# A sparse attention and ELU block on one core: the second batch's attention pieces placed by a written list, and the opening and the load queue reordered

## The chip, the cores and the metric

The kernel runs on one core of a Trainium2 chip. The metric is the device time of the program in microseconds (us). Three runs of the kernel before took 324.32, 326.67 and 323.88 us; their median is 324.32 us.

## What is computed

Two stages follow each other. First attention over 8 batches, 8 heads, 576 positions and 64 values a head: the first four heads see the last 32 positions ("local"), the other four see earlier positions that are equal modulo 32 ("strided"). Then the 4608 rows of 512 values go through two matrix products with an ELU between them.

```python
def _attn_ref(q, k, v):
    B, H, S, D = q.shape            # 8, 8, 576, 64
    stride = 32
    scores = 1.0 / np.sqrt(D) * np.matmul(q, k.transpose(0, 1, 3, 2))
    pos = np.arange(S)
    rel = pos[:, None] - pos[None, :]
    mask_local = (rel >= 0) & (rel < stride)
    mask_strided = (rel >= 0) & (pos[None, :] % stride == pos[:, None] % stride)
...
    attn = np.exp(scores)           # of the masked scores, less their maximum
    attn = attn / (np.sum(attn, axis=-1, keepdims=True) + 1e-09)
    return np.matmul(attn, v)

def _moe_ref(x, w_in, w_out):       # w_in 512 x 2048, w_out 2048 x 512
    h = x @ w_in
    g = np.where(h > 0.0, h, np.exp(np.minimum(h, 0.0)) - 1.0)
    return g @ w_out
```

## The kernel before

Everything is issued in an order written out by the program; the engines' queues run in that order, and each instruction waits only for what it needs. So a piece that waits holds up all that is queued behind it on its engine.

**Pairs and pieces.** A batch's attention is four pairs of heads: strided s0 and s1, local l0 and l1 (capital S0 and S1 are the strided pairs of batch 1). A pair is a chain of pieces: `t_q` and `t_k` transpose queries and keys on TensorE into a PSUM bank, from which ScalarE or VectorE copies them to SBUF (L360 to L387); `s0` and `s1` are the scores' matmuls with the exponential on ScalarE and the mask on VectorE (L488 to L525); `a0` and `a1` multiply with the values, and VectorE takes a reciprocal and a product (L527 to L555); `x` transposes the result back and copies it into `xT`, the ELU part's input (L566 to L595). `v_in` copies strided values from `v_raw` to `v_str` (L416), and `halo` copies the overlapping rows of local values within `v_loc` (L423); the local `a` pieces need it. In `xT` the four blocks of 128 rows are c = 0 (l0), 1 (l1), 2 (s0) and 3 (s1).

**PSUM.** `pair_a` holds scores, three single banks rotate through transposes, products and x ("the ring"), and three banks (two halves and the fourth single) rotate through the ELU's input products; late in a chunk the fourth single goes to the output products (`share`, L115).

**The opening** is batch 0's attention, written as the list `OPENING`. `fill.n` are n matmuls whose result nobody uses (L724); `moe.c` are the first three output blocks' matmuls for one block c of `xT` (L633). Pieces named in `ON_VECTOR` are copied by VectorE, all others of batch 0 by ScalarE.

**The chunks.** Then nine chunks of 512 rows follow. Chunk nb has 16 steps m: four matmuls with `w_in` (L629), the exponential on ScalarE (L655), and on VectorE a step with the exponential (L662) and a maximum with the product (L664); in chunk 0, m = 4, 7, 10, 13 and 15 have a ReLU on ScalarE instead (L658) and one VectorE step (L659). The output products (L678, `outs`) of a chunk run mostly during the next. Between these stand the attention pieces of batch nb + 1, at gaps: gap 2m is ahead of step m, gap 2m + 1 behind it. `attention` (L597) puts them there from a row of `TIMES`: a start, a pitch between pairs, and eight offsets. For batch 1 this was start 3, pitch 6: S0.t_k at gap 1, S0.s0 at 3, S0.a0 at 7, S1.halo at 13, l0.a0 at 19, l1.x at 30.

**Loads.** All loads but the first are issued by GpSimd in program order (L309 to L346, L738 to L746): among them quarter i of `w_in` (512 columns, steps 4i to 4i + 3), batch 1's strided q, k and v, its local q, k and v, then the third and fourth quarter of `w_in`, four pieces of `w_out`, some clears, and batch 2's loads.

Of the kernel before, what the change touches and what calls it, by code (L numbers as in the profile page):

```python
# [32 lines left out]
PIECES = (-2, -1, 0, 2, 3, 5, 7, 0)  # L33
TIMES = (
    None,
    (3, 6, (-3, -2, 0, 2, 4, 6, 9, 3)),
    (4, 6, (-3, -2, 0, 2, 4, 6, 8, 0)),
    (2, 7, PIECES),
    ((2, 8, 15, 22), 0, PIECES),
)  # L40

OPENING = """
s0.cast_q s0.t_q s0.t_k s1.cast_q s1.t_k s0.s0 s0.m0 s1.t_q s0.s1 s0.m1 fill.2 l0.t_q s1.s1
s1.m1 s1.s0 s1.m0 l0.t_k l1.t_q fill.1 s0.v l0.s0 l0.m0 l1.t_k l0.s1 s1.a0 s0.a0 l0.m1 l1.s0
s1.a1 s0.a1 fill.1 l1.s1 l1.m0 fill.1 s1.halo s1.x fill.1 s0.x l1.m1 fill.1 l0.a0 fill.1 l0.a1
l1.a0 moe.2 l1.a1 S0.t_q l0.x S1.t_q moe.3 l1.x moe.0 moe.1
""".split()  # L50
ON_VECTOR = "s0.t_q s1.cast_q s1.t_k l0.t_q s0.v l1.x".split()


ON_SCALAR = (4, 7, 10, 13, 15)
# [4 lines left out]
def kernel(  # L59
# [9 lines left out]
    nc = tc.nc  # L69
    B, H, S, D = q.shape  # L70
# [44 lines left out]
    def share(sc, hps, ops, ring):  # L115
        rings.update(sc=Ring(*sc), hps=Ring(*hps), ops=Ring(*ops), ring=Ring(*ring))
# [9 lines left out]
    def bf16_bank():  # L126
# [14 lines left out]
    v_str = [consts.tile([128, 4, 5, D + 1], BF16, tag=f"v_str{i}", name=f"v_str{i}")  # L141
             for i in range(3)]
# [23 lines left out]
    raw = {}  # L166
# [21 lines left out]
    def load_local(b, name):  # L188
        if name == "v":

            nc.gpsimd.dma_start(
                out=v_loc[b % 3][32:128, :, :, :D].rearrange("p h i d -> p (h i) d"),
                in_=v[b, 0:4].rearrange("h (i p) d -> p (h i) d", p=LB))
            return
        flat = nat[name, "loc"][b % 3]
        if b < EARLY:
            nc.gpsimd.dma_start(
                out=flat[0:LB].rearrange("p (h x) -> p h x", h=4),
                in_=src[name][b, 0:4].rearrange("h (p j) d -> p h (j d)", j=L_RUN))
            return  # L200
        t = flat[:, 0:20 * D].rearrange("p (a i e d) -> p a i e d", a=2, i=5, d=D)
        for h in range(4):
            nc.gpsimd.dma_start(  # L203
                out=t[:, h // 2, 0:4, h % 2],
                in_=src[name][b, h, 0:512].rearrange("(i p) d -> p i d", p=128))
        for a in range(2):
            nc.gpsimd.dma_start(
                out=t[0:64, a, 4],
                in_=src[name][b, 2 * a:2 * a + 2, 512:576].rearrange("h p d -> p h d"))

    def transpose_batch(b, local):

        def strided():
            for name, to in (("q", qT), ("k", kT)):
                nc.sync.dma_start_transpose(out=to["str"][b % 2],
                                            in_=nat[name, "str"][b % 3])

        if BY_DMA <= b <= LATE and local < 2:
            strided()
        if b >= EARLY and local:  # L220
            for name, to, o in (("q", qT, 0), ("k", kT, 32)):
                for a in range(2):
                    nc.sync.dma_start_transpose(
                        out=to["loc"][b % 2][:, a, o:o + 640].rearrange(
                            "p (i r) -> p i r", r=128),
                        in_=nat[name, "loc"][b % 3][:, 640 * a:640 * a + 640])
        if b > LATE:
            strided()

    def load_batch(b):  # L230
        for name in "qkv":
            load_strided(b, name)
        for name in "qkv":
            load_local(b, name)

    def rows_of(t, h):

        return t[0:126, h, 0:2, :], t[0:108, h, 2:5, :]
# [83 lines left out]
    def load_w_in(i):  # L322
        nc.gpsimd.dma_start(out=w_in_sb[:, :, 512 * i:512 * (i + 1)],
                            in_=wi[:, :, 512 * i:512 * (i + 1)])
# [5 lines left out]
    load_strided(1, "v")  # L330
    load_local(1, "q")
    load_local(1, "k")
    load_local(1, "v")
    load_w_in(2)


    class Pair:
# [6 lines left out]

        def copy(self, step, late):

            if self.b == 0:
                late = f"{self.name}.{step}" in ON_VECTOR
            return nc.vector.tensor_copy if late else nc.scalar.copy

        def cast(self, name):
# [214 lines left out]
        def x_out(self):  # L566
# [22 lines left out]
            else:  # L589
# [4 lines left out]
                        identity[0:LB, 0:LB])  # L594
                self.copy("x", self.b > 1)(dst, xt[:, 0:S])  # L595

    def attention(b, start, pitch, at):  # L597


        gaps = {}  # L600
        pairs = [Pair(b, s, hp) for s in (b < LATE, b >= LATE) for hp in range(2)]
        begin = start if b >= LATE else [start + pitch * i for i in range(4)]
        if b >= LATE:
            gaps[begin[0]] = [pairs[3].halo]
        for i, pr in enumerate(pairs):
            if b == 1 and pr.strided:
                pr.t_q = lambda: None
            for off, piece in ((at[0], pr.t_q), (at[1], pr.t_k),
                               (at[7], lambda pr=pr: pr.v_in(0)),
                               (at[7] + (b > 1), lambda pr=pr: pr.v_in(1)),  # L610
                               (at[2], lambda pr=pr: pr.scores(0)),
                               (at[3] if b < WHOLE else at[2] + (b < LATE),
                                lambda pr=pr: pr.scores(1)),
                               (at[4], lambda pr=pr: pr.av(0)),
                               (at[5] - (b >= LATE and i == 0),
                                lambda pr=pr: pr.av(1)),
                               (at[6] + (b > 1 and pr.strided) + (b >= LATE), pr.x_out), (at[5] - 2, pr.halo if b < LATE else lambda: None)):
                gaps.setdefault(begin[i] + off, []).append(piece)
        return gaps
# [91 lines left out]
    def run(gaps, keys):  # L711
        for gap in sorted(g for g in gaps if g in keys):
            for piece in gaps[gap]:
                piece()

    every = range(-10, 1000)
    pairs = {p.name: p for p in (Pair(0, s, hp) for s in (True, False) for hp in range(2))}
    pairs.update((f"S{hp}", Pair(1, True, hp)) for hp in range(2))
    parts = [s for s in OPENING if s.startswith("moe")]
    for step in OPENING:  # L720
        pair, what = step.split(".")
# [29 lines left out]
    def outs(nb, s):  # L751

        if nb == 0:
            return [(0, i) for i in range(3) if s == 11 + 2 * i]
        step = [(nb - 1, i) for i in range(3, MC)]
        if nb < n_chunks:
            step += [(nb, i) for i in range(3)]
        else:
            step[0:2] = step[1::-1]
        return step[s:s + 1]  # L760

    for nb in range(n_chunks + 1):

        if nb + 1 < B:
            gaps = attention(nb + 1, *TIMES[min(nb + 1, 4)])
            if nb == 0:
                share([pair_a], b_halves + singles[3:], [], singles[:3])
            elif nb + 1 < LATE:
                share([pair_a], b_halves, singles[3:], singles[:3])
            else:  # L770
                share([pair_a], b_halves + singles[:1], singles[3:], singles[1:3])
        else:
            gaps = {}
            share([], b_halves + singles[:1], singles[2:], singles[1:2])
        if nb + 3 < B:
            load_batch(nb + 3)
        for s in range(MC):
            if nb == 0 and s == 10:
                share([pair_a], b_halves, singles[3:], singles[:3])
            if s == (9 if nb + 2 > LATE else 6) and nb > 0 and nb + 2 < B:  # L780
                transpose_batch(nb + 2, int(nb + 2 >= LATE))
            if s == 13 and nb + 2 == EARLY:
                transpose_batch(nb + 2, 2)
            run(gaps, (2 * s,) if s else range(-10, 1))
            late = LATE <= nb + 1 and s + 1 < MC
            if nb < n_chunks:
                moe_in(nb, s)
            if nb < n_chunks and not late:
                moe_act(nb, s)
            run(gaps, (2 * s + 1,) if s + 1 < MC else range(2 * s + 1, 1000))  # L790
            if nb < n_chunks and late:
                moe_act(nb, s)
            if nb == B and s == 4:
                range_flag(row_ok16)
            for chunk, i in outs(nb, s):
                moe_out(chunk, i)
        if nb + 1 == B:
            row_ok16 = range_check()
# [163 lines left out]
```

## Time and profile before

| what | us |
|---|---|
| median of three runs | 324.32 |
| the profiled execution | 324.63 |
| its span, first to last instruction | 322.7 |
| TensorE matmuls busy | 304.5 |
| VectorE busy | 244.9 |
| ScalarE busy | 175.9 |
| GpSimd busy | 140.1 |

Times are from the start of the span. The profile's names: PE is TensorE's matmuls, PEld its weight loads, DVE is VectorE, ACT is ScalarE, POOL is GpSimd, SP is the queue that issues the output's transfers. `L629` is line 629 of the kernel before. In the timeline a line gives the start, the duration, the engine, the line, the operation with output and input, and in brackets how long the engine stood idle before and who ended that. A block of matmuls is shown with the last one's way through the array, so the next block may start before it ends. "Granted clock" is the share of full speed that TensorE was given.

Where the stages lie in the profiled execution: the opening to 27.3, chunk 0 from there to 55.8 (its first matmuls, the last `moe` of the opening, at 26.66), chunk 1 from 55.76 to 91.69.

### The profile page before, as it was taken

The numbers are of one execution on the slowest core, as the hardware profiler recorded it, in microseconds if no ns is written. First come the engines' busy times: TensorE is split into PE (matmuls) and PEld (weight loads), VectorE is DVE, ScalarE is ACT, GpSimd is POOL, SyncE is SP. The second block draws the span as 40 slices with busy tenths as digits, with TensorE's granted clock in tenths as the row PEclk, the third lists the DMA queues.
The fourth block names the chain that finished last, engine by engine and source line by source line (L and its number), as shares of the span: only waits on it lengthen the run. The fifth ranks groups of instructions, "written<-read, shape, count | busy, mean of one in ns | idle before, by whom it ended". The sixth has DMA issues, their size and how long they took to land.

```text
span 322.7 us, 6076 instructions
## 1 busy us (share of the span) xinstructions
PE 304.5 (94%) x2214; PEld 151.6 (47%) x2214; DVE 244.9 (76%) x539; ACT 175.9 (55%) x334; POOL 140.1 (43%) x218
## 2 busy tenths in 40 slices
PE   1997988999999999999999999999999999999994
PEld 0564444555544544444444444444444444444443
DVE  6576887787888988989798879887988566776610
ACT  3668885776555554555555565565555534434411
POOL 9859725958957839978942840000000000000000
PEclk9999899999999999999999999999999999999999
DMA  6999999999999999999994994291110000010012
GB/s 108 159 174 121 168 207 138 145 134 174 90 149 176 141 141 186 77 159 168 196 134 102 125 208 95 71 152 58 54 51 34 35 32 35 37 62 34 35 67 72
DMA packets 108970, 36.33 MB, mean 113 GB/s; under 512 B 87357, under 2 KB 104453, under 8 KB 108933
## 3 DMA queue, kind: packets, MB, share of 16 engines
q0 software_dynamic: 71632, 18.10, 62.4%
q1 hardware_dynamic: 37301, 17.77, 26.9%
q8 instruction: 19, 0.31, 0.4%
q14 instruction: 18, 0.15, 0.1%
HBM read 36.70 MB, written 9.44 MB: 143 GB/s over the span
## 4 chain that ended last, share of the span: by engine, by line
PE 85%; DVE 6%; ACT 3%; DMA 2%; issue 1%; POOL 1%; ACTq 0%; POOLq 0%
PE single L678 37%; PE half L629 27%; PE single L629 9%; PE single L542 3%; PE pair_a L463 2%; ACT e_sb L655 2%; PE single L382 2%; DMA k_str<-in_k_dram 2%; DVE g_sb L664 1%; DVE x_l L551 1%; PE single L578 1%; DVE e_sb L662 1%; PE single L368 1%; PE pair_a L500 1%; PE single L724 1%
## 5 line engine op out<-in xcount | busy, mean ns | idle before, releaser
L678 PE MATMUL single<-w_out_sb,g_sb 128*128 128x512 bf16 (+1 forms) x592 | 145.9, 373 | 0.0
L629 PE MATMUL half<-xT,w_in_sb 128*128 128x512 bf16 x436 | 113.4, 382 | 0.0
L655 ACT ACTIVATE e_sb<-half 128x512 f32<-128x512 f32 x109 | 65.3, 599 | 69.7 <-PE half L629 67.4
L662 DVE TENSOR_SCALAR e_sb<-e_sb 128x512 bf16<-128x512 f32 x139 | 64.0, 460 | 36.0 <-ACT e_sb L655 34.9
L678 PEld LDWEIGHTS <-g_sb 128*128 128x128 bf16 x592 | 55.2, 98 | 57.6 <-DVE g_sb L664 0.2
L629 PEld LDWEIGHTS <-w_in_sb 128*128 128x128 bf16 x576 | 52.0, 98 | 56.7 <-issue 2.2
L664 DVE TENSOR_TENSOR g_sb<-e_sb,half 128x512 bf16<-128x512 bf16 x104 | 71.5, 688 | 3.7
L629 PE MATMUL single<-xT,w_in_sb 128*128 128x512 bf16 x140 | 36.5, 379 | 0.0
L655 ACT ACTIVATE e_sb<-single 128x512 f32<-128x512 f32 x35 | 21.0, 600 | 24.2 <-PE single L629 22.0
L683 ACT COPY o_sb<-single 128x512 f32<-128x512 f32 (+1 forms) x37 | 21.3, 576 | 17.0 <-PE single L678 16.7
L542 PEld LDWEIGHTS <-pr 128*128 128x128 bf16 (+3 forms) x352 | 21.0, 106 | 15.6 <-issue 0.9
L469 ACT ACTIVATE pr<-pair_a 126x936 bf16<-126x936 f32 (+1 forms) x20 | 19.2, 962 | 12.5 <-PE single L463 12.5
L180 POOL DMA_DIRECT2D k_str<-in_k_dram x32 | 20.7, 662 | 10.7 <-DMA w_in_sb<-in_moe_w_in_dram 3.0
L664 DVE TENSOR_TENSOR g_sb<-e_sb,single 128x512 bf16<-128x512 bf16 x35 | 24.1, 688 | 1.2
L180 POOL DMA_DIRECT2D v_raw<-in_v_dram x32 | 19.9, 648 | 9.4 <-DVE v_str L421 7.5
L180 POOL DMA_DIRECT2D q_str<-in_q_dram x28 | 17.6, 650 | 6.4 <-DMA w_in_sb<-in_moe_w_in_dram 1.9
L551 DVE TENSOR_TENSOR x_l<-single,rden 96x384 bf16<-96x384 f32 x32 | 17.7, 553 | 1.1
L551 DVE TENSOR_TENSOR x_s<-single,rden 126x256 bf16<-126x256 f32 (+1 forms) x32 | 15.7, 491 | 1.1
L203 POOL DMA_DIRECT2D q_loc<-in_q_dram x20 | 15.5, 817 | 2.3 <-PE single L382 0.8
L203 POOL DMA_DIRECT2D k_loc<-in_k_dram x20 | 15.8, 820 | 0.7 <-DMA q_loc<-in_q_dram 0.5
L508 ACT ACTIVATE pr<-pair_a 128x576 bf16<-128x576 f32 (+2 forms) x20 | 13.0, 652 | 5.6 <-PE pair_a L500 5.5
L550 DVE RECIPROCAL rden<-single 96x6 f32<-96x6 f32 (+2 forms) x64 | 11.9, 185 | 3.3 <-PE single L542 2.7
(114 smaller groups left out, 261.6 us busy)
## 6 DMA issues: line engine op xcount, KB each, us to landing
out_dram<-o_sb SPq DMA_DIRECT2D x35, 256.0 KB, 3.1
v_loc<-in_v_dram POOLq DMA_DIRECT2D x8, 288.0 KB, 7.9
k_str<-in_k_dram POOLq DMA_DIRECT2D x32, 67.5 KB, 5.0
v_raw<-in_v_dram POOLq DMA_DIRECT2D x32, 67.5 KB, 4.7
w_in_sb<-in_moe_w_in_dram POOLq DMA_DIRECT2D x4, 512.0 KB, 10.0
w_out_sb<-in_moe_w_out_dram POOLq DMA_DIRECT2D x4, 512.0 KB, 16.5
q_str<-in_q_dram POOLq DMA_DIRECT2D x28, 67.5 KB, 7.2
q_loc<-in_q_dram POOLq DMA_DIRECT2D x20, 64.0 KB, 4.4
```

The lines of the kernel that those rows point to most:

```text
L180: engine.dma_start(out=t[0:108, h].rearrange("p g d -> p (g d)"), in_=rows[h, :, 0:30, :].rearrange("t (r g) d -> t r (g d)", g=5))
L203: nc.gpsimd.dma_start(out=t[:, h // 2, 0:4, h % 2], in_=src[name][b, h, 0:512].rearrange("(i p) d -> p i d", p=128))
L469: nc.scalar.activation(both, sc[0:nk, :, 0:w], ACT.Exp, scale=scale)
L508: nc.scalar.activation(halves, sc[0:nk, :, 0:w], ACT.Exp, scale=scale)
L542: nc.tensor.matmul(av[0:m, p, blk - b0, :], lhsT=pr[0:nk, o:o + m], rhs=vt[0:nk, 2 * self.hp + p, blk, :], start=True, stop=True)
L551: nc.vector.tensor_tensor(self.x[0:nq, b0:b0 + n].rearrange("q g p d -> q p g d"), av[0:nq, :, 0:n, 0:D], r.unsqueeze(3).to_broadcast([nq, ...
L629: nc.tensor.matmul(hps, lhsT=w_in_sb[:, c, m * 128:(m + 1) * 128], rhs=xT[:, c, nb * N_TILE:(nb + 1) * N_TILE], start=start, stop=stop)
L655: nc.scalar.activation(e_sb, hps, ACT.Exp)
L662: nc.vector.tensor_scalar(e1_sb, e_sb, scalar1=1.0, scalar2=1.0, op0=ALU.min, op1=ALU.subtract)
L664: nc.vector.tensor_tensor(g_of[nb][:, m, :], e1_sb, hps, op=ALU.max)
L678: nc.tensor.matmul(ops, lhsT=g_of[nb][:, m, kk * 128:(kk + 1) * 128], rhs=w_out_sb[:, m, cols], start=(m == 0), stop=(m == MC - 1))
L683: nc.scalar.copy(o_sb, ops)
```

## The change

`OPENING`: `s1.halo` stands ahead of l1.s1, `l0.a0` ahead of s0.x, `S0.t_q` behind `moe.3`, and two of eight fills are gone. S1.t_q's copy goes from ScalarE to VectorE. Batch 1's pieces in chunk 0 stand in a list, `SECOND`, with a gap for each, and no longer come from `TIMES`; its local pairs have their transposes there too. The copies of batch 1's strided values go from ScalarE, at gap 6, to GpSimd, in its queue behind the load of the local values. The third quarter of `w_in` is loaded ahead of the local values. Batch 2 starts at gap 5, not 4. The first three output pieces of chunk 0 follow steps 12, 14 and 15, not 11, 13 and 15, and the fourth single bank changes hands at step 11, not 10.

```diff
 TIMES = (
     None,
-    (3, 6, (-3, -2, 0, 2, 4, 6, 9, 3)),
-    (4, 6, (-3, -2, 0, 2, 4, 6, 8, 0)),
+    None,
+    (5, 6, (-3, -2, 0, 2, 4, 6, 8, 0)),
...
+SECOND = """
+3 S0.t_k 5 S0.s0 7 S0.s1 8 S1.t_k 9 S1.s0 11 S0.a0 11 S1.s1 12 S0.a1 13 S1.a0 14 l0.t_q
+15 S1.a1 15 S0.x 16 l0.t_k 17 l1.t_q 18 S1.x 18 l0.s0 19 l1.t_k 20 l0.s1 21 S1.halo 21 l1.s0
+22 l0.a0 24 l0.a1 24 l1.s1 26 l1.a0 26 l0.x 27 l1.a1 30 l1.x
+""".split()
...
-s1.a1 s0.a1 fill.1 l1.s1 l1.m0 fill.1 s1.halo s1.x fill.1 s0.x l1.m1 fill.1 l0.a0 fill.1 l0.a1
-l1.a0 moe.2 l1.a1 S0.t_q l0.x S1.t_q moe.3 l1.x moe.0 moe.1
+s1.a1 s0.a1 s1.halo fill.1 l1.s1 l1.m0 fill.1 s1.x l0.a0 l1.m1 fill.1 s0.x l0.a1 l1.a0 moe.2
+l1.a1 l0.x moe.3 S0.t_q l1.x S1.t_q moe.0 moe.1
 """.split()
-ON_VECTOR = "s0.t_q s1.cast_q s1.t_k l0.t_q s0.v l1.x".split()
+ON_VECTOR = "s0.t_q s1.cast_q s1.t_k l0.t_q s0.v l1.x S1.t_q".split()
...
     load_local(1, "k")
+    load_w_in(2)
     load_local(1, "v")
-    load_w_in(2)
+    for o, i in zip(rows_of(v_str[1][:, :, :, 0:D], slice(0, 4)),
+                    rows_of(raw[1], slice(0, 4))):
+        nc.gpsimd.tensor_copy(o, i)
...
-            if self.b == 0:
-                late = f"{self.name}.{step}" in ON_VECTOR
+            if self.b < 2:
+                name = self.name.upper() if self.b else self.name
+                late = f"{name}.{step}" in ON_VECTOR
             return nc.vector.tensor_copy if late else nc.scalar.copy
...
+    def second():
+        pairs.update((f"l{hp}", Pair(1, False, hp)) for hp in range(2))
+        gaps = {}
+        for gap, step in zip(SECOND[::2], SECOND[1::2]):
+            pair, what = step.split(".")
+            gaps.setdefault(int(gap), []).append(
+                lambda p=pairs[pair], what=what: p.step(what))
+        return gaps
...
-            return [(0, i) for i in range(3) if s == 11 + 2 * i]
+            return [(0, i) for i in range(3) if s == (12, 14, 15)[i]]
...
-            gaps = attention(nb + 1, *TIMES[min(nb + 1, 4)])
+            gaps = attention(nb + 1, *TIMES[min(nb + 1, 4)]) if nb else second()
...
-            if nb == 0 and s == 10:
+            if nb == 0 and s == 11:
                 share([pair_a], b_halves, singles[3:], singles[:3])
```

More of the change, by code (lines that the diff above doesn't have):

```diff
@@ L605, in attention @@
         for i, pr in enumerate(pairs):
-            if b == 1 and pr.strided:
-                pr.t_q = lambda: None
             for off, piece in ((at[0], pr.t_q), (at[1], pr.t_k),
```

## The prediction

> **What bounds the kernel now.** I began with the busy tenths over the span and the granted TensorE clock, from the profile's page.
>
> ```profile
> PE   1997988999999999999999999999999999999994
> ...
> PEclk9999899999999999999999999999999999999999
> ```
>
> One slice is 8.07 us. From the eighth slice on TensorE is full; what an order can win lies before 56 us, where the change's edits lie too. Busy time by stretch sharpens that (columns: PE, PEld, DVE, ACT, POOL busy with counts, clock, DMA share, GB/s):
>
> ```profile
> 16.00:24.00 8.00, 7.54 (x89) 4.96 (x86) 6.40 (x21) 5.29 (x11) 4.04 (x7) 1.00 1.29 174
> 24.00:32.00 8.00, 5.76 (x54) 3.43 (x54) 5.12 (x10) 6.58 (x12) 7.92 (x13) 0.95 1.01 120
> 32.00:40.00 8.00, 7.59 (x80) 4.04 (x77) 6.68 (x16) 6.43 (x13) 6.33 (x10) 0.84 1.63 167
> 40.00:48.00 8.00, 6.69 (x82) 3.59 (x77) 6.94 (x18) 6.96 (x15) 1.90 (x3) 1.00 1.24 207
> 48.00:56.00 8.00, 7.16 (x54) 3.68 (x53) 6.21 (x14) 5.00 (x9) 4.22 (x8) 1.00 1.04 143
> ```
>
> TensorE idles 0.46 + 2.24 + 0.41 + 1.31 + 0.84 = 5.3 us between 16 and 56, and in windows of 1 us the clock is 0.61, 0.50, 0.50, 0.68 from 31 to 35, which is 1.7 us of full clock lost. No engine is full: VectorE and ScalarE reach 87% at the densest, from 40 to 48. So the stage is bound by in-order queues waiting for each other. The timeline shows with whom:
>
> ```profile
> 24.01 0.41 PE L591 MATMUL single<-identity,x_l 96*128 96x96 bf16 x6 [0.24 <-DVE x_l L551]
> ...
> 24.70 0.43 PE L368 MATMUL single<-identity,q_str 126*128 126x126 bf16 x5 [0.28 <-DVE x_l L551]
> ...
> 28.52 0.28 PE L500 MATMUL pair_a<-qT_str,kT_str 64*128 64x126 bf16 x4 [0.78 <-ACT kT_str L371]
> ...
> 31.27 0.43 PE L542 MATMUL single<-v_str,pr 126*128 126x65 bf16 x4 [0.48 <-ACT v_str L421]
> ...
> 36.05 1.16 POOL L245 MEMSET q_str<- 32x1280 bf16 x1
> ...
> 36.72 0.77 DVE L662 TENSOR_SCALAR e_sb<-e_sb 128x512 bf16<-128x512 f32 x1
> ...
> 42.62 0.32 PE L578 MATMUL single<-identity,x_s 108*128 108x108 bf16 x3 [0.69 <-DVE x_s L551]
> ```
>
> Last, the landings of the third and fourth quarters of w_in:
>
> ```profile
> L323 POOL DMA_DIRECT2D w_in_sb<-in_moe_w_in_dram x2: 790/796/803, 29.7 to 30.4; - x2
> ...
> DMA to landing us min/median/max: 10.2/11.1/11.9
> ```
>
> 29.7 + 10.2 = 39.9 for the third quarter, and m=8, its first user, starts at 40.06: no slack. By the same view k_loc lands at 35.0, v_loc at 37.8, the fourth quarter at 42.3, w_out's pieces at 45.0, 47.5, 50.1 and 52.7: one after the other, with 203 to 213 GB/s from 37 to 51 us.
>
> **The opening.** Two of eight fills go. In place one takes 0.39 (19.04 to 19.43; 21.32 to 21.71), 0.78 for both; waits in the stretch are 0.23 + 0.24 + 0.28 = 0.75; so at most 1.5. Against it: the halo copy (1.27 on ScalarE) now stands ahead of l1.s1's exponential and delays it by 0.2 (19.14 to 19.33; v_loc landed by 18.1). I walked the new order with the old durations, three banks in rotation: l0.a0 at 19.9 (was 21.12), l1.a0 21.4 (22.29), moe.2 21.85 (22.48; its quarter lands at 21.5), VectorE's last product ends 23.65 (24.65), moe.1 starts 25.55 (26.66). Gain **1.1**, bounds 0.6 and 1.5. S1.t_q's copy (0.68 on ScalarE, 25.18 to 25.86) goes to VectorE (0.47 by the row of s0.t_q), idle from 24.65 to 26.15: nothing on the path, since ScalarE's first exponential waits for moe.1.
>
> **The list, to m=8.** Start to start, from the timeline: exponential 0.49, ReLU 0.48, local copies and exponentials 0.53, strided x copies 0.59; on VectorE the ELU's two steps 0.46 + 0.60, its ReLU form 0.61, a mask 0.36 to 0.41, reciprocal and product 0.67 to 0.70; four 512-column matmuls 0.86; m's first matmul to its exponential 1.13, exponential to VectorE 0.63. With S0.t_k at gap 3, S0.s0 waits for its copy behind exp1 (start 27.75, was 28.52), then TensorE has m=3 and S0.s1 to run on. VectorE from 26.7 on: six ELUs 6.36, two ReLU forms 1.22, four masks 1.54, four products 2.75, in all 11.9 with almost no wait, so S1.a1 ends at 38.7 (was 42.5, the halo among it). S0.x waits for a bank that S1.a0's product frees, 37.5; m=8 starts at 38.07 (was 40.06). The third quarter, now ahead of v_loc, lands 2.1 to 2.5 behind k_loc, at 37.1 to 37.5: it fits by half a microsecond. In the old order it would hold m=8 to 39.9.
>
> **From m=8 on.** ScalarE starts S0.x's copy at 37.95 and then has l0.t_k, exp8, l1.t_q, S1.x, l0.s0, exp9, l1.t_k, l0.s1, exp10, ReLU10 without a gap: end 44.0. S1.halo, now at gap 21, is queued on VectorE behind m=10's last step (44.0 to 44.6) and takes 0.49; l0.a0 needs it: 45.1, was 44.12. TensorE has only l1.s0 in hand from 42.62 to 45.13, so the halo costs 1.8. m=11 then starts 45.45 (46.21), m=15 53.1 (54.03), the next chunk 54.83 (55.76): gain 0.9, opening included; without the halo's wait 2.7. v_loc lands at about 40.1, under both. Between these ends I take 1.9: that wait hangs on ten ScalarE pieces in a row, and some follow each other closer (43.48 to 43.56 for the second x copy); 0.1 each brings 1.0 back.
>
> **The v copies on GpSimd.** Rows near: a memset of 1280 elements 1.16; this copy on ScalarE 0.63 + 0.83. I take 1.3, bounds 0.9 and 2.5. They start at 30.4 (v_raw lands by 30.2), ready 31.7; S0.a0, now at gap 11, wants them at 32.0, so beyond 1.6 they cost one for one, to 0.9. Queued behind them are the fourth quarter, w_out, the clears and batch 2's loads: 1.3 later issue, hidden because the transfers ahead run to 40. Beside that q_str memset VectorE's L662 took 0.77, where its median in this stretch is 0.44: 0.34 lost. The walk leaves VectorE 0.25 idle near 31.7, waiting for ReLU4, so **0.1** is charged, bounds 0 and 0.7. The Trainium skill (SBUF — State Buffer, "Who interferes with whom") says that GpSimd and some VectorE forms take one port pair exclusively, the later one waiting the whole instruction; it adds reads of two SBUF inputs, as the masks have, once GpSimd itself reads. The 0.77 agrees with the first; no row shows the second.
>
> **Outs, share, start 5.** The outs move behind one more gap; each is 0.86 wherever it stands. Its pieces have landed by then. m=10 takes the same bank in either ring, as all are old. Start 5 puts the second chunk's pieces one gap later; TensorE is full there, so nothing, save at its end: l1.x falls on gap 31, behind m=15, and its VectorE copy behind m=15's ELU. From m=15's first matmul the copy ends at 1.13 + 0.63 + 1.06 + 0.45 = 3.25; TensorE has m=15, the transposes, an out and three of four matmuls of the next m=0, 0.86 + 0.27 + 0.86 + 0.65 = 2.64. It waits **0.6**, and nothing later makes that good (bounds 0 and 0.7).
>
> **Sum.** 1.9 − 0.1 − 0.6 = 1.2. The profiled execution took 324.63 (span 322.7 and 1.9 around it), so 323.4; the three runs' median is 0.31 lower: **323.1**.
>
> **Rivals.** (a) The halo's wait throws the clock, and it is slower. Before 31 us TensorE was busy 1.53 of 3 us (27 to 30), and 3.4 us at half clock followed. In my walk 42.6 to 45.1 is emptier. With the full wait (gain 0.9 − 0.1 − 0.6 = 0.2) and half clock over m=11, m=12 and the first out, 1.7 of work is lost: 324.3 − 0.2 + 1.7 = **325.8**. It decides where TensorE's busy share over some 3.4 us falls to about half; against it, such a stretch may straddle two windows. The Trainium skill (TensorE: Matmul & The Clock Gate, Part 1) has the gate look at free-running windows of about 3.4 us; the trace's 3.4 us at half agrees, and which stretch is hit would then differ from run to run. Chance 0.17. (b) Every cover holds: no halo wait, no stall at the second chunk's end, 2.7 − 0.1: **321.7**. Its floor is batch 2's loads, pinned behind w_out (the k_str row pieces issue at 52.9, then v_raw to 57.9, landing about 60.6; its copy on VectorE, was second at 63.43, can come at most 2.8 earlier without waiting), so 320.9. For it: TensorE's 5.3 idle. Against: VectorE's 11.9 us in a row. 0.22. (c) The opening's gain becomes waiting on VectorE: full halo wait, 0.7 beside GpSimd, 0.6 at the end, −0.4: **324.7**. 0.14. My forecast, 322.2 to 324.2, keeps 0.47.
>
> A measurement of this kernel tells about 1% (3.2 us) from no change. Faster than 321.1 needs (b) and its floor: 0.09. Slower than 327.6 needs (a) with a second half-clock spell: 0.05. Within: 0.86. The range runs from (b)'s floor, 320.9, to (a), 325.8, leaving out half of (a) and the tails.
>
> **What would show it.** moe.1 near 25.5; m=8 near 38.1 with no wait for w_in; l0.a0 waiting on the halo copy of VectorE at about 43 to 45; the first out's piece at 47 or later; a wait at the second chunk's end on x_l's copy; clock rows between 26 and 50. I am wrong if S0.a0 waits for GpSimd, if m=8 waits for its quarter, or if batch 2's k_str stops TensorE after 55.

## The result, and the profile after

The changed kernel takes 329.21 us in the median of six runs (325.89, 326.62, 329.15, 329.28, 329.46, 330.04), the kernel before 324.51 in six beside it. The ratio is 1.0143, 95% interval 1.011 to 1.0177: slower by 1.4%, where I had forecast a gain of 0.4%. The measured time lies above my range. Here and below a ratio leaves out the few runs that are over 1.5% above the fastest of the same kernel (one of e6, two of the kernel before beside e9 to e11).

The profiled execution of the changed kernel took 325.89, with a span of 323.8; it is the quickest of its six. Its page, the same two rows as before:

```profile
PE   1878678999999999999999999999999999999994
...
PEclk9999989999999999999999999999999999999999
```

The thin slices are now the third, fifth and sixth from the start, and the half clock has moved from the fifth slice (31 to 35 us) to the sixth. The same stretches as before, with the same columns:

```profile
16.00:24.00 8.00, 6.14 (x93) 4.29 (x96) 7.09 (x22) 5.57 (x11) 5.43 (x10) 1.00 1.34 182
24.00:32.00 8.00, 6.55 (x62) 3.30 (x61) 6.53 (x12) 6.77 (x13) 7.53 (x11) 1.00 1.04 124
32.00:40.00 8.00, 5.59 (x81) 3.39 (x78) 6.67 (x17) 5.07 (x11) 7.59 (x12) 1.00 1.71 169
40.00:48.00 8.00, 5.66 (x57) 2.96 (x58) 5.52 (x11) 5.10 (x12) 2.29 (x4) 0.84 1.24 207
48.00:56.00 8.00, 7.06 (x56) 3.81 (x58) 6.18 (x14) 4.78 (x9) 4.56 (x8) 0.95 1.04 140
```

From 32 to 48 TensorE is busy 11.3 of 16 us, where it was 14.3. The timeline names the waits (columns as before; L646 is now the first product, L553 the product with the values, L602 the local x):

```profile
20.11 0.30 PE L553 MATMUL single<-v_loc,pr 128*128 128x65 bf16 x4 [0.67 <-ACT v_loc L439]
...
25.07 0.59 PE L646 MATMUL half<-xT,w_in_sb 128*128 128x512 bf16 x2
...
34.86 0.45 PE L393 MATMUL single<-identity,q_loc 96*64 96x96 bf16 x12 [1.14 <-DVE x_s L562]
...
37.57 0.41 PE L589 MATMUL single<-identity,x_s 126*128 126x126 bf16 x5 [1.08 <-DVE x_s L562]
...
38.29 1.04 PE L646 MATMUL single<-xT,w_in_sb 128*128 128x512 bf16 x4
...
45.57 0.40 PE L553 MATMUL single<-v_loc,pr 128*128 128x65 bf16 x4 [1.75 <-DVE v_loc L439]
45.78 1.90 PE L646 MATMUL half<-xT,w_in_sb 128*128 128x512 bf16 x4
...
92.44 0.30 PE L602 MATMUL single<-identity,x_l 96*128 96x96 bf16 x3 [0.51 <-DVE x_l L562]
```

The opening's last matmuls start at 25.07 (26.66 before), m=8 starts at 38.29 with no wait for its quarter of w_in, l0.a0 waits 1.75 for the halo copy, and m=11 right behind it runs at half clock, 1.90 for four matmuls. In the last line, at the end of chunk 1, l1.x of batch 2 waits for a product, where before it went through at once (89.70, 0.42 for all six).

| point reached, us | before | changed | changed, once more (e1) |
|---|---|---|---|
| moe.1 starts | 26.66 | 25.07 | 25.00 |
| chunk 1 starts | 55.76 | 56.27 | 55.11 |
| chunk 2 starts | 91.69 | 93.44 | 92.17 |
| span | 322.7 | 323.8 | 322.4 |

So in the profiled execution the opening gives 1.6, chunk 0 takes 2.1, chunk 1 1.2, and 0.65 comes back later, most of it a wait of 0.60 at 133.35 that the changed kernel's profile does not have. That makes 1.1, and the other runs are up to 4 us longer.

The 1.6 is not all due to the new opening. In both profiles TensorE begins slowly and speeds up, at different times; this is a fill of 512 columns near 18 us, before and changed:

```profile
18.13 0.61 PE L724 MATMUL single<-mask_l,identity 128*128 128x512 bf16 x1
```

```profile
18.20 0.39 PE L741 MATMUL single<-mask_l,identity 128*128 128x512 bf16 x1
```

Before, matmuls take the long time until 20.8; in the changed kernel's profile only until about 15. The granted clock is 1.00 there in both, so it does not show this. The section on the prediction compares like with like.

Part of what the longer runs hold shows in their granted clocks: with each run's span and mean clock, the time at half clock is 2 x (1 − clock) x span. It is 5.2, 2.6, 9.2, 3.3, 12.4 and 8.5 us for the six in the order of their times, where runs of the kernel before have 2.8 in the mean (the 73 runs beside the experiments below). A spell, below, is a stretch at half clock.

### The profile page after: what moved, and what is told of

The parts are those of the page before. It is cut to its first block, busy times and chain, and to the rows that moved or that the text cites. A ratio compares the mean times of both kernels' runs of the same rounds, so it can differ in the third digit from the quotient of the medians.

```text
span 323.8 us, 6033 instructions
## 1 busy us (share of the span) xinstructions
PE 298.6 (92%) x2171; PEld 150.0 (46%) x2212; DVE 245.4 (76%) x540; ACT 172.7 (53%) x331; POOL 140.3 (43%) x220
## 4 chain that ended last, share of the span: by engine, by line
PE 78%; DVE 10%; ACT 4%; POOL 3%; issue 2%; DMA 2%; ACTq 0%; DVEq 0%; POOLq 0%
PE single L695 36%; PE half L646 25%; PE single L646 9%; DVE g_sb L681 3%; PE single L553 3%; DVE e_sb L679 2%; PE pair_a L474 2%; DMA v_raw<-in_v_dram 2%; ACT e_sb L672 2%; DVE x_l L562 1%; PE single L589 1%; DVE x_s L562 1%; DVE pr L534 1%; POOL k_str L187 1%; PE single L602 1%
## 5 line engine op out<-in xcount | busy, mean ns | idle before, releaser
L695 PE MATMUL single<-w_out_sb,g_sb 128*128 128x512 bf16 (+1 forms) x571 | 142.8, 373 | 1.6 <-issue 0.8
L646 PE MATMUL half<-xT,w_in_sb 128*128 128x512 bf16 x424 | 111.7, 382 | 1.0 <-issue 0.5
L679 DVE TENSOR_SCALAR e_sb<-e_sb 128x512 bf16<-128x512 f32 x139 | 64.0, 460 | 37.5 <-ACT e_sb L672 36.9
L695 PEld LDWEIGHTS <-g_sb 128*128 128x128 bf16 x592 | 54.5, 98 | 56.3 <-DVE g_sb L681 0.4
L646 PEld LDWEIGHTS <-w_in_sb 128*128 128x128 bf16 x576 | 53.0, 98 | 57.8 <-issue 1.5
L646 PE MATMUL single<-xT,w_in_sb 128*128 128x512 bf16 x134 | 35.7, 379 | 0.3
L553 PEld LDWEIGHTS <-pr 128*128 128x128 bf16 (+3 forms) x352 | 20.5, 103 | 16.9 <-issue 3.6
L187 POOL DMA_DIRECT2D q_str<-in_q_dram x28 | 18.3, 679 | 5.3 <-DMA w_out_sb<-in_moe_w_out_dram 1.9
L210 POOL DMA_DIRECT2D k_loc<-in_k_dram x20 | 15.1, 776 | 1.2 <-issue 0.7
L553 PE MATMUL single<-v_loc,pr 128*128 128x65 bf16 x192 | 11.9, 198 | 2.8 <-DVE v_loc L439 1.8
```

The source lines that it names most:

```text
L187: engine.dma_start(out=t[0:108, h].rearrange("p g d -> p (g d)"), in_=rows[h, :, 0:30, :].rearrange("t (r g) d -> t r (g d)", g=5))
L210: nc.gpsimd.dma_start(out=t[:, h // 2, 0:4, h % 2], in_=src[name][b, h, 0:512].rearrange("(i p) d -> p i d", p=128))
L553: nc.tensor.matmul(av[0:m, p, blk - b0, :], lhsT=pr[0:nk, o:o + m], rhs=vt[0:nk, 2 * self.hp + p, blk, :], start=True, stop=True)
L646: nc.tensor.matmul(hps, lhsT=w_in_sb[:, c, m * 128:(m + 1) * 128], rhs=xT[:, c, nb * N_TILE:(nb + 1) * N_TILE], start=start, stop=stop)
L679: nc.vector.tensor_scalar(e1_sb, e_sb, scalar1=1.0, scalar2=1.0, op0=ALU.min, op1=ALU.subtract)
L695: nc.tensor.matmul(ops, lhsT=g_of[nb][:, m, kk * 128:(kk + 1) * 128], rhs=w_out_sb[:, m, cols], start=(m == 0), stop=(m == MC - 1))
```

## The experiments

Each is timed beside runs of the kernel before; ratios are to those. The runs are 4 to 12 each; e1 to e4 share 15 runs of the kernel before, e5 to e8 another 29, e9 to e11 another 29.

| run | what | ratio | 95% interval | mean us at half clock |
|---|---|---|---|---|
| e1 | changed kernel again | 1.0128 | 1.0093 to 1.0164 | 7.2 |
| e2 | S1.halo at gap 19 | 1.0068 | 1.0039 to 1.0097 | 4.5 |
| e3 | batch 2 from gap 4 | 1.0095 | 1.0061 to 1.0129 | 7.0 |
| e4 | values on ScalarE | 1.0101 | 1.0042 to 1.0161 | 3.6 |
| e5 | before, new opening | 0.9995 | 0.9965 to 1.0025 | 4.5 |
| e6 | changed, waits filled | 1.0058 | 1.0027 to 1.0090 | 1.9 |
| e7 | before, list and outs | 1.0107 | 1.0065 to 1.0148 | 4.7 |
| e8 | e2 and e3 together | 1.0020 | 0.9990 to 1.0051 | 3.5 |
| e9 | before, opening and load order | 0.9975 | 0.9946 to 1.0004 | 3.8 |
| e10 | e9, a wait filled | 0.9958 | 0.9936 to 0.9981 | 1.9 |
| e11 | e8, a wait filled | 1.0007 | 0.9978 to 1.0037 | 2.2 |

**e1, the changed kernel once more.** No edit.

> The changed kernel once more, nothing edited. The runs already taken fall in two groups, 325.9 to 326.6 and 329.2 to 330.0, and the trace of the first group is known: l0.a0 waits 1.75 us for the halo copy, a spell at half clock follows from 45.8, the next chunk's last local transposes wait for a product. Theory A (the halo and the clock spell make the loss, and the second group has one more clock spell): a run near 329.5 shows the same waits and two stretches of half clock. Rival B (a lock or a late load after 55 us): a run near 329.5 shows the same first 56 us and loses its 3 us later, in a wait on VectorE, on GpSimd or on batch 2's loads.

Five runs from 324.52 to 328.47; the traced one is the shortest. Its clock row from the page, and its wait from the list of what TensorE waited for (total us, times, longest):

```profile
PEclk9999999999999999999999999999999999999999
```

```profile
PE single L553 <- DVE v_loc L439: 1.8, 1, 1.8
```

The same wait of 1.8, and no half clock up to the last slice. So the wait is there without the spell behind it, and the spell differs from run to run of one program. From the start of m=8 to that of chunk 1 this trace takes 16.74 us (38.37 to 55.11), the kernel before 15.70. Three traces with the wait and a spell of about 3.4 us, the changed kernel's, e4's and e7's, take 17.95 to 18.01; e3's, with the wait and a spell of 6.8, takes 19.43. So the new order with its wait costs 1.0 here, and each 3.4 us at half clock 1.2 to 1.4 more. The other four runs have 5.2 to 11.1 us at half clock and take 2.5 to 4.0 us longer. No run near 329.5 was traced, so what was asked of such a run stays unanswered; rival B finds nothing in this trace after 56 us but the end of chunk 1.

GpSimd's copies are slower in this trace than in the changed kernel's profile, and TensorE waits for them:

```profile
30.93 2.94 POOL L344 COPY v_str<-v_raw 126x512 bf16<-126x512 bf16 x2
```

```profile
33.92 0.36 PE L553 MATMUL single<-v_str,pr 108*128 108x65 bf16 x6 [1.38 <-DVE g_sb L681]
```

The list of waits names a VectorE step that ends at the same moment, but S0.a1 does not need that step: in the changed kernel's profile it runs at 32.32, ahead of it. It needs the second copy, which ends at 33.87. The wait is made good before m=8, which starts at 38.37, 0.08 later than in the other profile.

**e2, the halo earlier.**

```diff
-18 S1.x 18 l0.s0 19 l1.t_k 20 l0.s1 21 S1.halo 21 l1.s0
+18 S1.x 18 l0.s0 19 l1.t_k 19 S1.halo 20 l0.s1 21 l1.s0
```

> The changed kernel with S1.halo at gap 19 (behind m=9) in place of 21 (behind m=10). Theory A: the wait of 1.75 us at l0.a0 goes but for some 0.3, the half clock spell behind it goes too, and the kernel gains 2.5 to 3.5 us on the changed one: 323 to 326.5 by group. Rival B (the loss lies after 55 us): it gains under 1 us, as the later stretch waits for batch 2's loads whatever comes before. Rival C (v_loc lands too late at 40.1): VectorE waits for v_loc at gap 19 and nothing is gained.

Against e1, by the ratios, it gains 0.6%, 1.9 us, under what I asked of theory A and twice rival B. The wait is 0.2 in its trace, so v_loc is there in time and rival C is out. But that trace is at half clock for about 6.8 us, now earlier, as its busy times by stretch show (the same columns, the clock third from the end):

```profile
36.00:40.00 4.00, 2.92 (x23) 1.34 (x20) 2.40 (x6) 2.32 (x5) 3.54 (x4) 0.62 2.44 134
40.00:44.00 4.00, 4.00 (x40) 1.95 (x39) 1.57 (x3) 2.65 (x6) 1.17 (x2) 0.53 1.24 207
```

Ahead of it lie the waits at l0.t_q and S0.x (1.2 and 1.1 here). The list has two thin stretches, and either can be hit.

**e3, batch 2 from gap 4.**

```diff
-    (5, 6, (-3, -2, 0, 2, 4, 6, 8, 0)),
+    (4, 6, (-3, -2, 0, 2, 4, 6, 8, 0)),
```

> The changed kernel with batch 2's pieces from gap 4 again, as before the change. My theory of the second chunk's end: l1.x back at gap 30 takes back the 0.5 us wait of its transposes and the wait of the next chunk's first block, 1.0 to 1.3 us in all, unless batch 2's keys, landing near 57, stop TensorE at S0.t_k, which then costs up to 1 us. Expected 0.5 to 1.3 us faster than the changed kernel. Rival: start 5 is what keeps TensorE from waiting for batch 2, then 0 to 1 us slower.

1.1 us better than e1 by the ratios and 0.6 by the medians, with intervals that overlap; the trace decides. Chunk 1 runs there from 58.05 to 93.97, 35.92 us; before 35.93; the changed kernel 37.17 and, in e1, 37.06. So start 5 costs 1.15 to 1.25. The end of the chunk in e3's timeline, TensorE alone:

```profile
91.98 0.42 PE L602 MATMUL single<-identity,x_l 96*128 96x96 bf16 x6
92.24 1.03 PE L646 MATMUL half<-xT,w_in_sb 128*128 128x512 bf16 x4
93.97 1.03 PE L646 MATMUL half<-xT,w_in_sb 128*128 128x512 bf16 x4
```

All six transposes go at once, ahead of m=15, and batch 2's keys did not stop TensorE.

**e4, the values on ScalarE.** GpSimd's two copies are taken out and `10 S0.v` is put in the list.

> The changed kernel with the copies of batch 1's strided values on ScalarE at gap 10 in place of GpSimd. Theory: GpSimd's copies took 1.6 us and stretched one VectorE mask and one ELU step by 0.4 and 0.6 us, but ScalarE pays 1.36 us for them near 31; the kernel stays within 0.7 us of the changed one. Rival: GpSimd's copies delay the issue of the fourth quarter, of w_out and of batch 2's loads and make the slower group; then the group near 329.5 is gone and the median falls by 3 us.

Four runs, 325.93 to 329.25: the time does not tell it from e1. A run of 329.25 is still there, and the median is 0.8 under e1's, not 3, which speaks against the rival. The timelines do show the port. The second mask of S0 with GpSimd's copies beside it (e1), and without (e4):

```profile
30.78 1.14 DVE L534 TENSOR_TENSOR pr<-pr,mask_w 108x648 bf16<-108x648 bf16 x1
```

```profile
31.31 0.49 DVE L531 TENSOR_TENSOR pr<-pr,mask_w 108x648 bf16<-108x648 bf16 x1
```

0.65 lost, on an operation with two inputs in SBUF, beside GpSimd's read of SBUF (its copies run from 30.93 to 33.87 in e1's trace). That is the second half of the rule of the Trainium skill (SBUF — State Buffer, "Who interferes with whom") that no row of before could show.

**e5, the opening alone.** The kernel before with the new `OPENING` and S1.t_q on VectorE.

> The kernel before with the changed opening list alone (S1.t_q on VectorE with it); batch 1's pieces, loads and outs as before. Theory: the opening's 1.1 to 1.6 us is real and the loss is all in the list, so this is the fastest so far, 0.8 to 1.8 us below the kernel before. Rival: the opening's gain turns into waiting in the old order (its third quarter of w_in lands at 39.9, and m=8 was there at 40.06), then within 0.5 us of before.

Rival: 0.9995. The traced run, 326.62, is the slowest of twelve that go down to 321.85; its TensorE timeline shows one way to lose the gain:

```profile
24.96 0.59 PE L630 MATMUL half<-xT,w_in_sb 128*128 128x512 bf16 x2
...
41.80 1.89 PE L630 MATMUL single<-xT,w_in_sb 128*128 128x512 bf16 x4 [2.55 <-DMA w_in_sb<-in_moe_w_in_dram]
```

moe.1 starts at 24.96, and m=8 then waits 2.55 for the third quarter, which lands later than the 39.9 of before, with half clock behind it. Whether the faster runs wait too is not shown.

**e6, the waits filled.** `15 fill.4` ahead of S0.x and `22 fill.8` ahead of l0.a0, each fill a matmul like those of the opening.

> The changed kernel with four idle 512-column matmuls ahead of S0.x and eight ahead of l0.a0, where TensorE waits 1.1 and 1.75 us; they fill these waits and compute nothing used. Theory: these thin stretches bring the half clock, of which the changed kernel's runs show 7.0 us in the mean and those of before 3.1; with them filled the mean falls to 4 or less and the time by 1 to 2 us against the changed kernel. Rival: the clock spells come from elsewhere, or cost nothing because VectorE and ScalarE set the pace, then no change, or up to 0.5 slower where a fill overhangs its wait.

Mean time at half clock 1.9 for 7.2 in e1, and the ratio falls by 0.7%, 2.3 us (each against its own runs of the kernel before). Fills make no work faster, so I put this down to the clock, some 2 us. The clock is not the whole spread: the eleven runs in the ratio still go from 323.45 to 327.21, and the 327.21 has 0.7 us at half clock.

**e7, the list alone.** The kernel before with `SECOND` (`6 S0.v` added) and the outs at 12, 14, 15; start 4, opening and loads as before.

> The kernel before with the list for batch 1 and the later outs alone: old opening, old order of loads, values copied on ScalarE at gap 6, batch 2 from gap 4. Theory: the list alone carries the loss, 1 to 3 us slower than before; l0.a0 waits for the halo copy as in the changed kernel. Rival: the loss needs the loads or start 5 as well, then within 0.7 us of before.

1.0107, 3.5 us, and its trace has the same 1.8 at l0.a0. But the loss is not the list's alone, for this run has a wait that the changed kernel does not have:

```profile
32.59 0.28 PE L508 MATMUL pair_a<-qT_str,kT_str 64*128 64x126 bf16 x4 [2.25 <-ACT kT_str L379]
```

ScalarE's copy of the values, at gap 6, waits until 29.52 for them to land, and all behind it on ScalarE is late. So m=8 starts at 40.09, no earlier than before, where the changed kernel has 38.29.

**e8, halo and start together.** Both edits of e2 and e3.

> The changed kernel with both S1.halo at gap 19 and batch 2 from gap 4. Each alone took about 1 to 2 us off (medians 325.9 and 327.0 where the changed kernel had 327.7). Theory: they add, as they lie in different chunks: 324.5 to 325.5, still not below before, because the two waits for S0.a0's and S1.a0's products (1.1 us each) stay. Rival: with the halo's wait gone, batch 2's keys and values land too late for gap 4 and the second gain is lost: as with the halo alone.

They add: 1.0020 where the changed kernel has 1.0128, 3.5 us back with two small moves, and the two intervals do not meet.

**e9, opening and load order.** The kernel before with the new opening, and:

```diff
     load_local(1, "k")
+    load_w_in(2)
     load_local(1, "v")
-    load_w_in(2)
...
-(at[5] - 2, pr.halo if b < LATE else lambda: None)
+(at[5] - 2 + 4 * (b == 1), pr.halo if b < LATE else lambda: None)
```

> The kernel before with the changed opening list and the third quarter of w_in ahead of the local values; S1.halo four gaps later (17), since those values now land near 40; all else as before. With the opening alone m=8 waited 2.55 us for that quarter, and nothing was gained. Theory: opening and load order are one gain of 1.0 to 1.6 us together, and the list is what loses: 322.2 to 322.9 where before has 323.8. Rival: the order of before cannot use the lead, as VectorE sets the pace there too: within 0.5 us of before.

323.14 beside 324.41 in the medians, less than hoped in the ratio (0.8 us), and the interval just takes in no change. No wait for w_in is left in its trace.

**e10, with a wait filled.**

```diff
+        if b == 1:
+            gaps.setdefault(2, []).append(lambda: [
+                nc.tensor.matmul(pair_a[:, 0], lhsT=identity, rhs=mask_l[:, 0:512],
+                                 start=True, stop=True) for _ in range(3)])
         return gaps
```

> The same, with three idle 512-column matmuls at gap 2 into the score bank, between S0.t_k and S0.s0, where TensorE waits 0.8 us for ScalarE's copy and then again for its exponential. They compute nothing used. Theory of the clock: the stretch from 26 to 31 brings the half clock in some runs of this order; filled, the mean time at half clock falls below 2 us and the median by 0.3 to 0.8 us against the same kernel without fills. Rival: no fewer spells, or S0.s0 comes later behind the fills, 0 to 0.4 us slower.

The time at half clock halves, from 3.8 to 1.9. The median does not fall (323.25); the ratio, 0.9958, is lower than e9's within both intervals. So the clock part holds, the time part is not settled. But this version is faster than both kernels: 1.4 us below before, with an interval that ends at 0.9981.

**e11, the mended list with a wait filled.** e8 and `15 fill.4`.

> The changed kernel with the halo at gap 19, batch 2 from gap 4, and four idle matmuls ahead of S0.x. Theory: without the fills this had 3.4 us at half clock in the mean and a median 0.83 us above before; the fills halve the clock time and bring the median to within 0.3 us of before, 323.3 to 324.2. Rival: the spells stem from the wait ahead of l0.t_q, which the fills leave, then as without them, 324.3 to 325.

Half clock 2.2 for 3.5, ratio 1.0007 for 1.0020: in the expected direction, and too small to tell; the median, 324.83 beside 324.41, lies in the rival's range. Its trace has a late load behind 56 us: VectorE waits for batch 2's strided values,

```profile
63.81 0.43 DVE L432 COPY v_str<-v_raw 126x512 bf16<-126x512 bf16 x1 [3.24 <-DMA v_raw<-in_v_dram]
```

and TensorE waits 1.1 behind it (0.7 in e10's trace). Both have batch 2 from gap 4, so e3's rival can hold in single runs.

## Why the prediction was wrong

**The opening** gained, but not the 1.6 that the two profiles show, nor the 1.1 of the walk. I sort the traces by the time at which TensorE speeds up and take the start of chunk 0's first exponential. Where it speeds up by 15 us, the old opening has 25.88 (e7) and seven traces of the new one 24.63 to 25.55, 25.23 in the mean. Where it does so after 20, the old one has 27.14 (before) and four of the new one 26.05 to 27.00, 26.45 in the mean. Either way the list gives about 0.7, an estimate, as each group has one trace of the old opening; the rest of the 1.6 is TensorE's speed. The fill was mis-sized too: 0.39 is read at 19.04, where TensorE was still slow, while at full speed four such matmuls take 0.86.

**m=8** started at 38.29 for 38.07, with no wait for its quarter; in e5's trace, without the reorder, it waits 2.55, and in e3's, with it, still 0.53. **The walk from m=8 on** was right in its first version: l0.a0 at 45.57 for 45.1, the wait 1.75 for 1.8, and from m=8 to chunk 1 16.76 walked (38.07 to 54.83), 16.74 in e1, the trace without a spell.

The step that failed is the choice behind it: "Between these ends I take 1.9". I had the full wait as one end, then gave 1.0 back because some ScalarE pieces follow each other closer. Nothing of it came back: every trace with the halo at gap 21 and nothing filled shows 1.75 or 1.8. The one row that I leaned on is a short second copy, not a piece of the usual kind. In the profiled execution chunk 1 starts at 56.27, where the 1.9 taken puts it at 53.86: 0.97 is what I took back, 0.47 is l0.a0 later than walked, and 0.97 lies behind l0.a0, where the spell is. The clock is the second step that failed: the sum puts it at nothing and leaves it to rival (a). My number for the profiled execution was 323.4, and it took 325.89; the median lies 6.1 above its forecast, so it holds more than this trace shows.

**Rival (a)**, at 0.17, is what the profiled execution shows: the full wait, half clock behind it, 325.89 for 325.8. The median of 329.21 is not explained by it alone; it was undersized in two ways. I priced one spell behind the halo's wait; the list has a second thin stretch ahead of l0.t_q and S0.x, where the prediction has S0.x waiting for its bank until 37.5 without putting that beside the clock; and a spell can be 6.8 us long (e2, e3). The changed kernel's runs have 4.2 us more at half clock than those of before, worth 2.1 of full-speed work; e6's 2.3 is near it, and so is the 1.2 to 1.4 for each 3.4 us that the traces under e1 give, 1.5 to 1.7 for 4.2.

**The second chunk's end** cost 1.15 to 1.25, not 0.6. I had counted the copy behind m=15's ELU, but l1.x's transposes wait too: the product of l1.a1 now stands behind m=14's ELU on VectorE, and only one block and one out lie between (0.51 and 0.61 of waiting in the two traces).

**GpSimd's copies** took 1.60 in the changed kernel's profile, not 1.3, and 2.94 in e1's, above my bound of 2.5. VectorE lost 0.65 on one mask there, where I charged 0.1. S0.a0 did not wait, but S0.a1 did, 1.38 in e1. I had also called no engine full, and GpSimd, whose queue got the copies, was busy 7.92 of 8 us from 24 to 32. Whether the copies cost time in the end is open (e4).

The floor of rival (b) does not follow from its own numbers: 324.3 less 2.8 is 321.5, not 320.9. The result lies far above it.

Together: the halo's wait 1.9 (e2), start 5 1.1 (e3), the rest of the list, its outs and GpSimd's copies about 1.5, from e8 at 1.0020 against e9's 0.9975; the opening and load order give 0.8 back. That is 3.7 of the 4.1 us that e1 lost, each term a difference of ratios and uncertain by about 1 us; the clock is inside these terms, not beside them. What is shown is the pair: with the halo and batch 2 moved back (e8), 3.5 us return. Which part of the list loses the 1.5 is not shown. The opening and the load order together are probably a gain (e9); e10, which fills a wait as well, is clearly one.

One thing stays open: the run of 329.28 had only 3.3 us at half clock, so not all of the slower runs is the clock, and no trace caught a run near 329.5. Two things vary from trace to trace without showing in the granted clock: the opening's speed, worth 1.2 on chunk 0's start, and a wait for a product of x_l in chunk 3, 0.9 in e2's trace, 0.6 in e4's and none in the changed kernel's. Whether they make the slow runs is not shown.

## What to carry to other kernels

When a walk of the queues gives a wait in full, charge it in full, unless a row shows the same chain going faster. An empty stretch on TensorE has two prices, the wait itself and the clock behind it, so moving waits together can cost more than their sum; look at the granted clock of every run, not of the profiled one alone. Before two profiles are compared at the start of a program, compare the durations of the same matmul in both. And when a list is delayed by one gap, walk its last piece against the next chunk's first need.

## What the runs showed of the hardware

TensorE can start slowly for longer than its first few microseconds, and for a different time in each traced run, with a granted clock of 1.00: a 512-column fill takes 0.61 and later 0.38 to 0.39, and the change comes between 12.9 and 23.0 us in these 13 traces. What sets the time is not shown.

VectorE can be held far longer than one GpSimd instruction. In the changed kernel's timeline an ELU step that takes 0.43 took 1.82, beside a row of six short memsets by GpSimd (two of the six shown):

```profile
59.96 1.82 DVE L679 TENSOR_SCALAR e_sb<-e_sb 128x512 bf16<-128x512 f32 x1 [0.85 <-ACT e_sb L672]
```

```profile
59.79 0.44 POOL L257 MEMSET q_loc<- 32x256 bf16 x1
60.04 0.44 POOL L257 MEMSET k_loc<- 32x256 bf16 x1
```

The memsets start every 0.25 us up to 61.05, and the step ends at 61.78, 0.29 after the last memset's end. In seven more traces (e1 to e6 and e8) the step takes 1.07 to 1.94, begins at other times, and ends 0.27 to 0.29 after the last one's end. Before, the third memset starts 0.54 after the second, not 0.25, and the step, 1.10 long, ends between the two. No wait of TensorE is put down to it in either profile, but it is 1.4 us of VectorE for six clears.
